# A float32 stage of a tuned FFT-convolution and MLP kernel, remade as three float32r products whose moving halves are split on ScalarE and VectorE

## The chip, the cores and the metric

The kernel runs on one core of one Trainium2 chip. The metric is the device time of one execution in microseconds (us); lower is better.

## The reference, cut to what matters

```python
X = np.fft.rfft(x, axis=1)                      # x: 8 x 3008 x 256, float32
Y = X * (filt_r + 1j * filt_i)[None, :, :]
y = np.fft.irfft(Y, n=3008, axis=1)
h = y.reshape(8 * 3008, 256) @ w_in             # 256 x 2048
P = a[0] + a[1] * h + a[2] * h**2 + a[3] * h**3
Q = 1.0 + abs(b[0]) * abs(h) + abs(b[1]) * h**2
out = (P / (Q + 1e-6)) @ w_out                  # 2048 x 256
```

## The kernel before, in words

The length 3008 is 64 x 47. A batch's convolution has three stages. Stage 1 is the 47-point transform: inputs are folded (a sum or a difference of two mirrored halves, `fold`) and multiplied on TensorE by a 120 x 120 constant (`half_sb`). Stage 2 is the 64-point transform, the filter and the way back. Stage 3 is the inverse 47-point transform, which writes `xhl`, the input of the MLP, as a high and a low float32r part.

The MLP runs over 47 tiles of 512 tokens and, in each, 16 slices of 128 hidden features: a *unit*, 753 in all (the last two steps are halved). A unit has six matmuls into `h_u` (L706 to L709, `product_in`), the rational function on ScalarE, VectorE and GpSimd, and six matmuls out of `hi_u` and `lo_u` (L797 to L799, `product_out`). The names in the rows:

- ScalarE: `act0` L714 (reads `h_u`, writes `q_u`), `act4` L739, `act2` L727, `act1` L721, `act3` L731, five of 128x512 a unit.
- VectorE: `g_hi` L763, `rest` L771, `p` L754, `g_lo` L777, four a unit; each has `h_u`, which lies in PSUM, as one input and an SBUF tile as another.
- GpSimd: `pool_m` L768 and `pool_q1` L749, two a unit, all operands in SBUF.

All compute engines run in the order in which the program is written (`manual_schedule`), and an iteration of the loop in `pipeline` writes out the parts of several units: `in` of unit i, a step of the convolution on TensorE, `out` of an older unit, `g_hi` of i-2, `act3` of i-1, `act0` of i, the convolution step's work on the other engines (`conv_out`), `act4` of i-1, `act2` and `act1` of i, `rest` of i-3, `p` of i-1, `g_lo` of i-3, `pool_m` of i-2, `pool_q1` of i-1. A step of the convolution is let in when a credit of 0.38 an iteration has paid for the step before; its cost is the number that the generator yields (0.86 for a half of stage 1).

The second batch's stage 1 (`stage1`, `b == 1`) and that of the third to eighth (`b` of 2 to 7) are the same generator. It has 13 steps, two for each of six input tiles and one for the seventh. In a step TensorE multiplies one folded half in plain float32 (L519), ScalarE writes the high part (L473, over the input tile `xin`), VectorE the low part (L475, tile `yl`, reads PSUM and `xin`), GpSimd folds the half that is needed two steps later (L456, tile `xs`), and after a tile's last half two DMAs store it. PSUM has six banks (`Banks`) for `h_u` and the convolution; the bank free for longest is taken next.

Rings of SBUF tiles (`RING`) hold the units' values: `q=5` lets `act0` of unit i write a tile that `rest` of unit i-5 was the last to read.

`product3` (L422) multiplies two operands, each given as a high and a low float32r part, by three matmuls: high x high, low x high, high x low. Stage 2 uses it already.

Of the kernel before, what the change touches and what calls it, by code (L numbers as in the profile page):

```python
# [9 lines left out]
F32 = mybir.dt.float32  # L10
F32R = mybir.dt.float32r
I32 = mybir.dt.int32
U32 = mybir.dt.uint32
AF = mybir.ActivationFunctionType
ALU = mybir.AluOpType
# [12 lines left out]
R0 = NB * K2  # L28
SW = 448
AB = 432  # L30
C = 256
# [3 lines left out]
RATES = 0.6, 0.38  # L35
EARLY = 60
XF = 1
RING = dict(a=4, w=3, q=5, hi=5, lo=4)
GAP = 4
PGAP, XGAP = 1, 1  # L40
OG = 2
# [5 lines left out]
XB, FB, YB = 4, 3, 3  # L47
# [9 lines left out]
REST = 2  # L57
# [2 lines left out]
WARM2 = (3, 3, 3, 3)  # L60
DUE = 5
SPN = 1
HEAD_SP = {mybir.EngineType.SP}
SQ0 = 624
SQP = "PA"
# [3 lines left out]
TT = 512  # L69
# [58 lines left out]
class Plan:  # L128
# [10 lines left out]
    def add(self, name, fn, engine, busy, after=(), due=0.0, moves=0.0, bank=None, ring=None, twin=None, then=(), filler=False, pick=None):  # L139
        self.steps.append((name, fn, engine, busy, list(after), due, moves, bank, ring, twin, then, filler, pick))  # L140
# [49 lines left out]
def conv_moe(ctx: ExitStack, tc: tile.TileContext, xp, filt, w_in, w_out, mats, small, sgn, outT):  # L190
    nc = tc.nc
    B = xp.shape[0]

    consts = ctx.enter_context(tc.tile_pool(name="consts", bufs=1))
    dram = ctx.enter_context(tc.tile_pool(name="dram", bufs=3, space=DRAM))
    conv = ctx.enter_context(tc.tile_pool(name="conv", bufs=2))
    mlp = ctx.enter_context(tc.tile_pool(name="mlp", bufs=1))
# [9 lines left out]
    fwd32_sb = consts.tile([128, 128], F32, name="fwd32_sb")  # L207
    small_sb = consts.tile([128, SW], F32, name="small_sb")
    half_sb = [small_sb[:R0, h * R0 : h * R0 + R0] for h in range(2)]
    e_sb = small_sb[:, 2 * R0 : 2 * R0 + 4 * N2]  # L210
    scal = consts.tile([128, 64], F32, name="scal")
    ab_sb, abs_sb, cf_sb = small_sb[:, AB : AB + 12], scal[:, 12:24], scal[:, 24:40]
# [3 lines left out]
    ts, tt, stt = v.tensor_scalar, v.tensor_tensor, v.scalar_tensor_tensor  # L216
# [105 lines left out]

    slots = [f"{x}{k}" for k in range(5) for x in ("a", "w", "q", "hi", "lo") if k < RING[x]]

    class Weights:
# [12 lines left out]
        def load(self):  # L338
            i = self.i
            tag = self.tag  # L340
            bufs = {"raw": 1, "xin": XB, "f1": FB, "f2": FB}.get(tag)
            if tag == "tl":
                raw = conv.tile([128, 4 * C], U32, tag=tag, name=f"raw{i}").rearrange("p (c t) -> p c t", t=2)
            else:
                raw = conv.tile([128, TT, 2], U32, tag=tag, name=f"raw{i}", **({"bufs": bufs} if bufs else {}))
            self.l, self.h = raw[:, :, 0], raw[:, :, 1]
            nc.sync.dma_start(raw.rearrange("p c t -> p (c t)"), self.src)
# [71 lines left out]
    def product3(out, parts, hi, lo):  # L419

        for n, (a, b) in enumerate(((0, hi), (1, hi), (0, lo))):
            nc.tensor.matmul(out, parts[:, a], b, start=n == 0, stop=n == 2)  # L422

    class Banks:
# [6 lines left out]
        def tile(self, name):  # L431
            k = min(self.free, key=self.free.get)
            del self.free[k]
            return k, ps.tile([128, TT], F32, tag=f"h{k}", name=name)
# [6 lines left out]
    def width(t):  # L441
        return TT if t < 6 else C

    def stage1_load(b, t, tile=None):
        n = width(t)
        if tile is None:
            tile = conv.tile([128, 2, n], F32, tag="xin", name=f"xin{b}_{t}", bufs=XB)
        nc.sync.dma_start(
            tile.rearrange("p a b -> p (a b)"),
            xp[b, 2 * TT * 128 * t : (2 * TT * t + 2 * n) * 128].rearrange("(p c) -> p c", p=128),  # L450
        )
        return tile

    def fold(engine, h, out, xin):

        engine.tensor_tensor(out=out, in0=xin[:R0, 0], in1=xin[:R0, 1], op=(ALU.add, ALU.subtract)[h])  # L456

    def stage1_store(issuer, b, t, parts):

        n = width(t) // C  # L460
        for of, part in zip(parts, range(2)):
            slots = scr1[b][part].rearrange("k (b j) r c -> (k b) j r c", j=NJ)[:, 2 * t : 2 * t + n]
            of = of if of.dtype == F32 else of.bitcast(F32)
            issuer.dma_start(slots.rearrange("p j r c -> p (j r c)"), of[:R0, : 2 * n * C])

    def stage1_evict(t, h, parts, pt):

        if t < 6:
            in_ = pt[:R0].rearrange("p (j c) -> p j c", j=2)
            hi, *low = (of[:R0].rearrange("p (j r c) -> p j r c", j=2, r=2)[:, :, h] for of in parts)  # L470
        else:
            in_, (hi, *low) = pt[:R0], (of[:R0, :TT] for of in parts)
        nc.scalar.activation(hi, in_, AF.Copy)  # L473
        for lo in low:
            tt(out=lo, in0=in_, in1=hi.bitcast(F32), op=ALU.subtract)  # L475

    def half_dfts(t, h):
        return [(h, slice(0, TT))] if t < 6 else [(g, slice(g * C, g * C + C)) for g in range(2)]

    def stage1(b, t0=0):  # L480
        tiles, xins = {}, {}

        def load(t):
            if t < 7:
                xins[t] = stage1_load(b, t)

        def prepare(t, h):
            if t > 6:
                return
            if h == 0:  # L490
                load(t + 1)
                xin, n = xins.pop(t), width(t)
                sums = conv.tile([R0, 2, n], F32, tag="ev", name=f"xs{b}_{t}")
                tiles[t] = sums, xin
            sums, xin = tiles[t]
            fold(nc.gpsimd, h, sums[:, h], xin)

        load(t0)
        for _ in range(REST if b == 1 else 1):
            yield 0.01  # L500
            yield
        for h in range(2):
            prepare(t0, h)
            yield
        yield 0.01
        yield
        for t in range(t0, 7):
            sums, xin = tiles.pop(t)
            flat = xin.rearrange("p a b -> p (a b)")
            if b == 1:  # L510
                parts = (flat,)
            else:
                low = conv.tile([128, 4 * C], F32R, tag="yl", name=f"yl{b}_{t}", bufs=YB)
                parts = flat.bitcast(F32R), low
            for h in range(2 if t < 6 else 1):
                yield 0.86
                k, pt = banks.tile(f"s1_{b}_{t}_{h}")
                for g, cs in half_dfts(t, h):
                    nc.tensor.matmul(pt[:R0, cs], half_sb[g], sums[:, g], start=True, stop=True)  # L519
                yield  # L520
                stage1_evict(t, h, parts, pt)
                banks.done(k, 0.5)
                prepare(t + 1, h)
            stage1_store(nc.sync, b, t, parts)

    class Stage2:

# [159 lines left out]
    class Unit:  # L687
# [7 lines left out]
        def tile(self, tag, dt=F32):  # L695
            full = mlp.tile([128, TT], dt, tag=f"{tag}{self.i % RING[tag]}", name=f"{tag}_u{self.i}")
            return full[:, self.cols]
# [103 lines left out]
    banks = None  # L801
# [19 lines left out]
    whole, parts = slice(0, T), [slice(c, c + T // LAST) for c in range(0, T, T // LAST)]  # L821
# [1 line left out]
    units[-TAIL:] = [(t, f, c) for t, f, _ in units[-TAIL:] for c in parts]  # L823

    def conv_items(b):
        yield from stage1(b)
        for _ in range(GAP):
            yield
        yield from stage2(b)
# [6 lines left out]
    def head():  # L836
# [3 lines left out]
        first, sums, pts, yts, zts, pair = {}, {}, {}, {}, {}, []  # L840
# [10 lines left out]
            nc.sync.dma_start(sgn_sb[:, :K2], sgn)  # L851

        def load_pair():
            tile = mlp.tile([128, TT], F32, tag=slots[20], name="pair")
            nc.sync.dma_start(tile, mats.rearrange("p m c -> p (m c)"))
            pair.extend(tile[:, k * 128 : k * 128 + 128] for k in range(4))

# [118 lines left out]
        add = plan.add  # L976
        due = lambda i: DUE + 2.6 * i
        for t in range(7):
            add(f"x{t}", lambda t=t: x_load(t), "SP", 0.5, due=-20 + t, moves=1.55 if t < 6 else 0.78, ring=(("xin", "xin", "xin", "xin", "oe", "oe", "tl")[t], f"sum{min(2 * t + 1, 12)}"))
            if t == 0:  # L980
                add("small", lambda: nc.sync.dma_start(small_sb, small), "SP", 0.5, due=-19.5, moves=0.7)
        add("mats", load_mats, "SP", 0.5, due=-10, moves=0.05)
        add("pair", load_pair, "SP", 0.5, due=-9, moves=0.8)
        add("fwd32", load_fwd32, "SP", 0.5, ["s12"], due=60, moves=0.2)
        add("mats_upper", mats_upper, "ACT", 0.97, ["pair", "sev12"], due=45)
# [30 lines left out]
        for k, i in enumerate(FIRST):  # L1016
            w, n = weights[i], f"w{i}"
# [19 lines left out]
        def split():  # L1037
            nonlocal xh, xl
            xhl = consts.tile([128, 4, RX], F32R, tag="xhl", name="xhl")
            xh, xl = xhl[:, :2], xhl[:, 2:]  # L1040
# [24 lines left out]
    def pipeline(squares):  # L1065
# [10 lines left out]
        for i in range(n + LAG + 2 * OG):  # L1076
# [10 lines left out]
            if i == 0:  # L1087
                sp.enter_context(tc.manual_schedule(engines=HEAD_SP))
            for k in SOON.get(i, ()):
                weights[k].load()  # L1090
            if i == SPN:
                sp.close()
# [86 lines left out]
    with tc.manual_schedule(engines=ENGINES):  # L1179
        with tc.manual_schedule(engines=HEAD_SP):  # L1180
            banks = Banks(range(8 - T * 2 // TT))
# [85 lines left out]
```

## Time and profile before

| | |
|---|---|
| median of 3 runs | 2452.14 us (2450.94 to 2453.37) |
| the profiled execution | 2452.45 us, span 2450.3 us |
| TensorE clock granted | 0.999 |
| TensorE, VectorE, ScalarE, GpSimd busy | 99%, 89%, 91%, 87% |

The span is the time from the first to the last instruction; the 2.15 us around it belong to the execution's time but to no engine. Busy time is the union of an engine's instructions. A matmul's end is modelled and reaches into the next matmul's start, so TensorE's pace is read from the distance between starts; the same holds for ScalarE and VectorE where one instruction follows another without idle time.

### The profile page before, as it was taken

The numbers are of one execution on the slowest core, as the hardware profiler recorded it, in microseconds if no ns is written. First come the engines' busy times: TensorE is split into PE (matmuls) and PEld (weight loads), VectorE is DVE, ScalarE is ACT, GpSimd is POOL, SyncE is SP. The second block draws the span as 40 slices with busy tenths as digits, with TensorE's granted clock in tenths as the row PEclk, the third lists the DMA queues.
The fourth block names the chain that finished last, engine by engine and source line by source line (L and its number), as shares of the span: only waits on it lengthen the run. The fifth ranks groups of instructions, "written<-read, shape, count | busy, mean of one in ns | idle before, by whom it ended". The sixth has DMA issues, their size and how long they took to land.

```text
span 2450.3 us, 36825 instructions
## 1 busy us (share of the span) xinstructions
PE 2419.5 (99%) x10868; PEld 1949.4 (80%) x10868; DVE 2188.6 (89%) x3554; ACT 2231.9 (91%) x4275; POOL 2138.8 (87%) x2240
## 2 busy tenths in 40 slices
PE   9899999999999999999999999999999999999998
PEld 5578778888788887888788877888788888888887
DVE  7988988999899988998899988889899998998998
ACT  6899999999999999999899999999999999888887
POOL 7889987999789987999779997899879987889898
PEclk9999999999999999999999999999999999999999
DMA  7543344333443234432343334333343210100000
GB/s 263 174 130 97 104 137 133 111 90 94 127 145 106 87 108 132 125 104 81 113 158 106 98 99 133 126 100 94 100 133 117 64 38 18 34 26 17 21 9 20
DMA packets 127502, 243.30 MB, mean 99 GB/s; under 512 B 10803, under 2 KB 75763, under 8 KB 127291
## 3 DMA queue, kind: packets, MB, share of 16 engines
q1 hardware_dynamic: 127207, 240.77, 31.8%
q8 instruction: 88, 1.44, 0.3%
q14 instruction: 123, 1.01, 0.1%
q10 hardware_dynamic: 84, 0.08, 0.0%
HBM read 149.47 MB, written 91.34 MB: 98 GB/s over the span
## 4 chain that ended last, share of the span: by engine, by line
PE 72%; POOL 14%; DVE 7%; issue 4%; ACT 2%; DMA 1%; SPq 0%; POOLq 0%; DVEq 0%; ACTq 0%
PE o L798 10%; PE o L797 10%; PE o L799 10%; PE h_u L706 10%; PE h_u L707 10%; PE h_u L709 10%; POOL q_u L768 6%; POOL q_u L749 4%; PE x L665 3%; PE s L519 3%; DVE h_u L771 2%; POOL zw L580 2%; PE z L422 2%; DVE hi_u L763 1%; DVE h_u L754 1%
## 5 line engine op out<-in xcount | busy, mean ns | idle before, releaser
L768 POOL TENSOR_TENSOR q_u<-q_u,hi_u 128x512 f32<-128x512 f32 x753 | 977.0, 1297 | 198.2 <-DVE hi_u L763 174.8
L771 DVE SCALAR_TENSOR_TENSOR h_u<-h_u,q_u 128x512 f32<-128x512 f32 x753 | 523.0, 695 | 124.7 <-POOL q_u L768 123.4
L797 PE MATMUL o<-hi_u,wo_sb 128*128 128x512 f32 x1506 | 633.5, 421 | 0.0
L706 PE MATMUL h_u<-xhl,wi_sb 128*128 128x512 f32 x1506 | 590.9, 392 | 9.7 <-DVE lo_u L777 4.5
L798 PE MATMUL o<-lo_u,wo_sb 128*128 128x512 f32 x1506 | 587.8, 390 | 3.7 <-DVE lo_u L777 3.7
L799 PE MATMUL o<-hi_u,wo_sb 128*128 128x512 f32 x1506 | 586.6, 390 | 0.1
L707 PE MATMUL h_u<-xhl,wi_sb 128*128 128x512 f32 x1506 | 586.1, 389 | 0.2 <-DVE xhl L681 0.2
L749 POOL TENSOR_SCALAR q_u<-q_u,scal 128x512 f32<-128x512 f32 x753 | 580.8, 771 | 4.1 <-ACT a_u L731 4.1
L714 ACT ACTIVATE q_u<-h_u 128x512 f32<-128x512 f32 x753 | 451.6, 600 | 134.1 <-PE h_u L709 105.7
L754 DVE SCALAR_TENSOR_TENSOR h_u<-w_u,scal,h_u 128x512 f32<-128x512 f32 x753 | 563.4, 748 | 3.2 <-ACT w_u L721 3.2
L763 DVE SCALAR_TENSOR_TENSOR hi_u<-h_u,a_u 128x512 fp32r<-128x512 f32 x753 | 515.2, 684 | 3.7 <-ACT a_u L739 3.4
L777 DVE TENSOR_TENSOR lo_u<-h_u,a_u 128x512 fp32r<-128x512 f32 x753 | 516.9, 686 | 0.3
L731 ACT ACTIVATE a_u<-q_u 128x512 f32<-128x512 f32 x753 | 477.8, 635 | 0.0
L727 ACT ACTIVATE q_u<-q_u 128x512 f32<-128x512 f32 x753 | 472.9, 628 | 1.8
L709 PE MATMUL h_u<-xhl,wi_sb 128*128 128x512 f32 x1506 | 463.7, 389 | 0.0
L721 ACT ACTIVATE w_u<-h_u 128x512 f32<-128x512 f32 x753 | 446.3, 593 | 0.0
L739 ACT ACTIVATE a_u<-a_u 128x512 f32<-128x512 f32 x688 | 433.1, 629 | 0.3
L706 PEld LDWEIGHTS h_u<-xhl,wi_sb 128*128 128x128 f32 x1506 | 282.6, 188 | 80.2 <-DVE lo_u L777 16.3
L798 PEld LDWEIGHTS o<-lo_u,wo_sb 128*128 128x128 f32 x1506 | 283.3, 188 | 79.4 <-issue 20.9
L797 PEld LDWEIGHTS o<-hi_u,wo_sb 128*128 128x128 f32 x1506 | 282.9, 188 | 74.4 <-issue 20.5
L799 PEld LDWEIGHTS o<-hi_u,wo_sb 128*128 128x128 f32 x1506 | 282.7, 188 | 60.7 <-POOL wo_sb L401 0.5
L707 PEld LDWEIGHTS h_u<-xhl,wi_sb 128*128 128x128 f32 x1506 | 282.7, 188 | 59.2 <-issue 0.7
(125 smaller groups left out, 2262.3 us busy)
## 6 DMA issues: line engine op xcount, KB each, us to landing
f<-filt SPq DMA_DIRECT2D x168, 256.0 KB
xin<-xp SPq DMA_DIRECT2D x48, 512.0 KB
scr<-ev SPq DMA_DIRECT2D x47, 512.0 KB
outT<-oe SPq DMA_DIRECT2D x46, 512.0 KB
xin<-scr SPq DMA_DIRECT2D x42, 512.0 KB
scr<-xin SPq DMA_DIRECT2D x42, 480.0 KB
yl<-scr SPq DMA_DIRECT2D x36, 512.0 KB
tl<-scr SPq DMA_DIRECT2D x94, 192.0 KB
```

Of the source, the lines that this page charges most:

```text
L706: nc.tensor.matmul(o, w_in_part(0, f, cc), xh[:, cc, ts], start=cc == 0, stop=False)
L707: nc.tensor.matmul(o, w_in_part(0, f, cc), xl[:, cc, ts], start=False, stop=False)
L709: nc.tensor.matmul(o, w_in_part(1, f, cc), xh[:, cc, ts], start=False, stop=cc == 1)
L749: nc.gpsimd.tensor_scalar(out=self.q, in0=self.q, scalar1=S1, scalar2=S2, op0=ALU.mult, op1=ALU.add)
L754: v.scalar_tensor_tensor(out=H, in0=w, scalar=PK, in1=H, op0=ALU.add, op1=ALU.mult)
L763: nc.vector.scalar_tensor_tensor(out=self.hi, in0=self.H, scalar=self.p0, in1=self.a, op0=ALU.add, op1=ALU.mult)
L768: nc.gpsimd.tensor_tensor(out=self.q, in0=self.q, in1=self.hi.bitcast(F32), op=ALU.mult)
L771: nc.vector.scalar_tensor_tensor(out=self.H, in0=self.H, scalar=self.p0, in1=self.q, op0=ALU.add, op1=ALU.subtract)
L777: nc.vector.tensor_tensor(out=self.lo, in0=self.H, in1=self.a, op=ALU.mult)
L797: nc.tensor.matmul(o, w_out_part(0, f, dd), self.hi, start=f == 0 and self.cols.start == 0, stop=False)
L798: nc.tensor.matmul(o, w_out_part(0, f, dd), self.lo, start=False, stop=False)
L799: nc.tensor.matmul(o, w_out_part(1, f, dd), self.hi, start=False, stop=f == 15 and self.cols.stop == T)
```

## The change

Stage 1 of batches three to eight has a generator of its own, `stage1_parts`. Its folds go to a new ring of two float32 tiles (`sh`). One step ahead of its use each folded half is split: ScalarE copies it into a float32r tile (high part), VectorE subtracts that from the folded half (low part). Both operands of this subtraction and its result lie in SBUF. The constant is split likewise, once, into `half_r`, 2,048 bytes of a partition. The float32 matmul becomes `product3`. The ring `q` goes from five tiles to four, and `pair`, a constant of the head, moves into a tile of `sh`.

```diff
-RING = dict(a=4, w=3, q=5, hi=5, lo=4)
+RING = dict(a=4, w=3, q=4, hi=5, lo=4)
+SH = 2
+    half_r = consts.tile([128, 2, 2, 128], F32R, name="half_r")
...
-        for _ in range(REST if b == 1 else 1):
+        for _ in range(REST):
...
+    def half_parts():
+        f = small_sb[:R0, : 2 * R0].rearrange("p (h c) -> p h c", h=2)
+        hi, lo = (half_r[:R0, k, :, :R0] for k in range(2))
+        nc.scalar.activation(hi, f, AF.Copy)
+        tt(out=lo, in0=f, in1=hi.bitcast(F32), op=ALU.subtract)
+
+    def stage1_parts(b):
+        xins, sums, parts, low = {}, {}, {}, {}
+        last = 12
...
+        def add(k):
+            if k > last:
+                return
+            t, h = divmod(k, 2)
+            if h == 0:
+                load(t + 1)
+            sums[k] = conv.tile([R0, TT], F32, tag="sh", name=f"sh{b}_{k}", bufs=SH)
+            for g, cs in half_dfts(t, h):
+                fold(nc.gpsimd, g, sums[k][:, cs], xins[t])
+
+        def split(k):
+            if k > last:
+                return
+            x = sums.pop(k)
+            parts[k] = tile = conv.tile([R0, 2, TT], F32R, tag="ev", name=f"xs{b}_{k}")
+            nc.scalar.activation(tile[:, 0], x, AF.Copy)
+            tt(out=tile[:, 1], in0=x, in1=tile[:, 0].bitcast(F32), op=ALU.subtract)
+
+        load(0)
+        if b == 2:
+            half_parts()
+        yield 0.01
+        yield
+        add(0)
+        yield
+        split(0)
+        add(1)
+        yield
+        yield 0.01
+        yield
+        for k in range(last + 1):
+            t, h = divmod(k, 2)
+            yield 0.86
+            bank, pt = banks.tile(f"s1_{b}_{t}_{h}")
+            tile = parts.pop(k)
+            for g, cs in half_dfts(t, h):
+                w = half_r[:R0, :, g, :R0]
+                product3(pt[:R0, cs], w, tile[:, 0, cs], tile[:, 1, cs])
+            yield
+            if h == 0:
+                low[t] = conv.tile([128, 4 * C], F32R, tag="yl", name=f"yl{b}_{t}", bufs=YB)
+            out = xins[t].rearrange("p a b -> p (a b)").bitcast(F32R), low[t]
+            stage1_evict(t, h, out, pt)
+            banks.done(bank, 0.5)
+            split(k + 1)
+            add(k + 2)
+            if h or k == last:
+                stage1_store(nc.sync, b, t, out)
...
-        yield from stage1(b)
+        yield from stage1(b) if b == 1 else stage1_parts(b)
...
-            tile = mlp.tile([128, TT], F32, tag=slots[20], name="pair")
+            tile = conv.tile([128, TT], F32, tag="sh", name="pair", bufs=SH)
```

## Rows read from the trace of the kernel before

**Rows 1.** The page's part 1: busy us of each engine, share of the span, instructions.

```profile
PE 2419.5 (99%) x10868; PEld 1949.4 (80%) x10868; DVE 2188.6 (89%) x3554; ACT 2231.9 (91%) x4275; POOL 2138.8 (87%) x2240
```

**Rows 2.** Timeline of TensorE in batch three's stage 1: start, length, engine, line.

```profile
363.00 0.39 PE L706 MATMUL h_u<-xhl,wi_sb 128*128 128x512 f32 x1
363.23 0.39 PE L707 MATMUL h_u<-xhl,wi_sb 128*128 128x512 f32 x1
...
365.72 0.39 PE L706 MATMUL h_u<-xhl,wi_sb 128*128 128x512 f32 x1
...
367.08 1.02 PE L519 MATMUL s<-xs,small_sb 120*120 120x512 f32 x2
...
369.32 0.39 PE L706 MATMUL h_u<-xhl,wi_sb 128*128 128x512 f32 x1
```

**Rows 3.** Busy time in the six stage-1 stretches of batches three to eight.

```profile
331.20:407.80 76.60, 76.38 (x329) 59.14 (x328) 66.79 (x108) 69.49 (x132) 59.50 (x58) 1.00 0.36 112
...
sum 443.90, PE 443.05 PEld 342.02 DVE 387.13 ACT 404.04 POOL 351.01; mean PE 73.84 PEld 57.00 DVE 64.52 ACT 67.34 POOL 58.50
```

**Rows 4.** Groups of instructions by line and shape: busy us, mean ns, idle before.

```profile
L456 POOL TENSOR_TENSOR xs<-xin 120x512 f32<-120x512 f32 x84 | 108.7, 1293 | 0.0
...
L519 PE MATMUL s<-xs,small_sb 120*120 120x512 f32 x168 | 86.4, 594 | 2.6 <-DVE raw L390 1.2 <-DVE yl L475 0.9 <-DVE lo_u L777 0.5
...
L475 DVE TENSOR_TENSOR yl<-s,xin 120x512 fp32r<-120x512 f32 x78 | 53.9, 691 | 46.5 <-ACT xin L473 46.5
L590 ACT ACTIVATE zr<-f 128x512 fp32r<-128x512 f32 x84 | 52.9, 630 | 9.2 <-POOL f L584 8.2
```

**Rows 5.** Timeline of ScalarE in the same stretch.

```profile
364.68 0.60 ACT L714 ACTIVATE q_u<-h_u 128x512 f32<-128x512 f32 x1
365.16 0.64 ACT L739 ACTIVATE a_u<-a_u 128x512 f32<-128x512 f32 x1
365.68 0.64 ACT L727 ACTIVATE q_u<-q_u 128x512 f32<-128x512 f32 x1
```

**Rows 6.** Timeline of VectorE in the same stretch.

```profile
362.78 0.69 DVE L475 TENSOR_TENSOR yl<-s,xin 120x512 fp32r<-120x512 f32 x1 [1.71 <-ACT xin L473]
363.38 0.69 DVE L771 SCALAR_TENSOR_TENSOR h_u<-h_u,q_u 128x512 f32<-128x512 f32 x1
...
365.24 0.68 DVE L763 SCALAR_TENSOR_TENSOR hi_u<-h_u,a_u 128x512 fp32r<-128x512 f32 x1
...
367.69 0.68 DVE L763 SCALAR_TENSOR_TENSOR hi_u<-h_u,a_u 128x512 fp32r<-128x512 f32 x1
368.77 0.69 DVE L475 TENSOR_TENSOR yl<-s,xin 120x512 fp32r<-120x512 f32 x1 [0.40 <-ACT xin L473]
```

**Rows 7.** Timeline of GpSimd in the same stretch.

```profile
361.62 1.30 POOL L768 TENSOR_TENSOR q_u<-q_u,hi_u 128x512 f32<-128x512 f32 x1
362.90 0.78 POOL L749 TENSOR_SCALAR q_u<-q_u,scal 128x512 f32<-128x512 f32 x1
...
369.35 1.29 POOL L768 TENSOR_TENSOR q_u<-q_u,hi_u 128x512 f32<-128x512 f32 x1
```

**Rows 8.** Timeline of VectorE in the head of the kernel.

```profile
7.89 6.96 DVE L456 TENSOR_TENSOR xs<-xin 120x512 f32<-120x512 f32 x12 [2.55 <-DMA xin<-xp]
...
21.01 0.83 DVE L377 TENSOR_SCALAR wp<-wt 128x512 uint32<-128x512 uint32 x1
```

**Rows 9.** Timeline of GpSimd in the head of the kernel.

```profile
7.42 0.19 POOL L242 TENSOR_TENSOR scal<-scal 128x1 f32<-128x1 f32 x1
...
8.78 0.48 POOL L245 TENSOR_TENSOR scal<-scal 128x6 f32<-128x6 f32 x1
...
11.71 0.67 POOL L250 TENSOR_TENSOR scal<-scal 128x2 f32<-128x2 f32 x1
```

**Rows 10.** The view of waits: us in total, times, longest us.

```profile
DVE yl L475 <- ACT xin L473: 46.5, 66, 2.1
...
PEld h_u L706 <- DVE lo_u L777: 16.3, 30, 1.7
```

More of the change, by code (lines that the diff above doesn't have):

```diff
@@ L509, in stage1 @@
             flat = xin.rearrange("p a b -> p (a b)")
[L510 to L514, printed above, removed]
+            parts = (flat,)
             for h in range(2 if t < 6 else 1):
@@ L524, in stage1, with load @@
             stage1_store(nc.sync, b, t, parts)
+    def half_parts():
[6 more added lines that the diff above has]
+        last = 12
+        def load(t):
+            if t < 7:
+                xins[t] = stage1_load(b, t)
+        def add(k):
[44 more added lines that the diff above has]
+                stage1_store(nc.sync, b, t, out)
     class Stage2:
```

## Prediction

> **What bounds the kernel now.** I read the page's busy shares first. TensorE is busy for 99% of the span, VectorE, ScalarE and GpSimd for 89, 91 and 87% [rows 1]: one engine leads and three follow closely, so time taken off TensorE counts only as far as the next engine has room. A busy TensorE is not yet a TensorE at its pace, so the timeline came next. In batch three's stage 1 matmuls start 0.23 us apart (363.00, 363.23), the twelve of a unit without a convolution step take 365.72 - 363.00 = 2.72 us, and a unit with a stage-1 half takes 369.32 - 365.72 = 3.60 us [rows 2]. TensorE works without a gap there and sets the pace; a float32 half costs it 3.60 - 2.72 = 0.88 us. (The 594 ns in the view by line are the modelled length of one of its two records [rows 4] and are no price.)
>
> The change touches six stretches, the stage 1 of batches three to eight, 78 halves. I measured them together: 443.9 us, in which TensorE is busy for 443.1, ScalarE for 404.0, VectorE for 387.1, GpSimd for 351.0 [rows 3]. The room is thus 39.9 us on ScalarE, 56.8 on VectorE, 92.9 on GpSimd. The change sends work to the first two.
>
> **What it takes off TensorE.** Three float32r matmuls at 0.227 us (2.72 / 12) are 0.68 us, against 0.88: 0.20 us a half. The seventh tile has two 256-column pieces, six short matmuls for four; I count it like the others, six of 78. Together 78 x 0.20 = 15.6 us: TensorE then needs 443.9 - 15.6 = 428.3 us in the six stretches. The third weight load of a half runs beside the matmuls, as the unit's loads do.
>
> **What it adds to ScalarE.** A copy of 120x512 from SBUF to SBUF for each half. The nearest row is L590, the same copy for stage 2: 0.63 us by itself [rows 4]; in a row ScalarE instructions start 0.48 and 0.52 us apart [rows 5], so 0.52: 78 x 0.52 = 40.6. Need: 404.0 + 40.6 = 444.6 us. That is too high by as much as the instructions now end in idle time: the first stretch has 132 in 69.49 us [rows 3], 0.526 each, and one after the other they take about 0.51. At that the old ones need 404.0 x 0.51 / 0.526 = 391.7 and all 432. So 432 to 445, 437 taken.
>
> **What it adds to VectorE.** A 120x512 subtraction a half. L475 lasts 0.69 us [rows 4] and the next instruction follows 0.60 us after its start (362.78, 363.38) [rows 6]: 78 x 0.60 = 46.8, need 387.1 + 46.8 = 433.9 us. The 46.5 us in which VectorE now waits at L475 for ScalarE's high part [rows 10] lie inside its idle time; they shrink when VectorE is the late one, since ScalarE's copy is then done, so I add nothing for them. With that alone both engines would need a little more than TensorE (428) and less than now (443.9).
>
> **The port.** The new subtraction is unlike every other VectorE instruction of these stretches: those have an operand in PSUM, it has both in SBUF. The trace has such instructions in its head: twelve folds by VectorE, back to back from 7.89 to 14.85 [rows 8]. GpSimd's tiny instructions take 0.19 us just before; beside the folds they take 0.48 and 0.67, the step of the folds (6.96 / 12 = 0.58) [rows 9]. So GpSimd waits there for a VectorE instruction with two SBUF inputs. In the other direction one row hints at it: an instruction of VectorE with SBUF on both sides lasted 0.83 us at 21.01 [rows 8], where 0.69 is usual for its size; GpSimd was at work on SBUF then. The Trainium skill (SBUF — State Buffer, "Who interferes with whom") states the rule: a VectorE instruction with two SBUF inputs and a GpSimd instruction that reads SBUF exclude each other, and whichever starts first holds the shared pair for its whole length. By that rule the sum is the forecast below; without it, it is the first rival. The trace agrees for GpSimd's side.
>
> In these stretches GpSimd is busy for 351.0 of 443.9 us, and its instructions are long. How long would the subtraction wait? It comes right behind L475. At least nothing; at most a whole L768, 1.28 us (361.62 to 362.90) [rows 7]. Two places can be read off. At 363.38 it would find L749 at work until 362.90 + 0.78 = 363.68: 0.30 us. At 368.77 + 0.60 = 369.37 L768 has just begun, 1.26 us to go [rows 6, 7]. In the second VectorE came late by only 0.40 us of waiting for ScalarE. Once VectorE sets the pace, the phase can be worked out: GpSimd starts L768 when L763 is done, then L749, then the fold, 1.28 + 0.78 + 1.29 = 3.35 us [rows 4, 7]; VectorE's next L763 is done 2.45 us later (365.24, 367.69), L475 takes 0.60, so the subtraction is ready at 3.05 and waits for 0.30 us [rows 6]. I take 0.30, where the calculation and the first place meet: 78 x 0.30 = 23.4, and VectorE needs 433.9 + 23.4 = 457.3 us. Half of a long instruction, 0.64, would make it 484; nothing, 433.9. GpSimd loses up to 0.60 us a half, 47 us, and has 92.9.
>
> So VectorE takes TensorE's place as the bound: 457.3 - 443.9 = 13.4 us more. Not all of it reaches the end. VectorE may leave a stretch late and catch up in stage 2, where it has room (its share over the span is 89%). How late is limited by the ring.
>
> **The ring of four.** `act0` of unit i must now come after `rest` of i-4 instead of i-5. At 364.68 it follows the `rest` that ended at 363.38 + 0.69 = 364.07, by 0.61 us [rows 5, 6]; that is the slack that is left, where the ring of five had a unit's time more. As long as VectorE is no later than now it costs nothing: the distance covers it. Behind the waiting `act0` stand ScalarE's high part of the convolution and `act4`, which VectorE wants next, so a VectorE later by more than 0.6 us holds ScalarE as well. I credit 0.6 us for each stretch, 6 x 0.6 = 3.6. A second limit is close to it: TensorE's first matmul of a unit already waits for L777 to free a bank, 16.3 us in 30 places [rows 10], and the subtraction puts every L777 behind it 0.6 us later.
>
> **At nothing.** The folds stay on GpSimd, same number, same time of issue; only their tile changes. Each half is split a step, two iterations, after its fold, so ScalarE finds it done. The stores and loads are the same and stand where they stood in SP's queue. `half_parts` is one small instruction on each of two engines, once. `pair` changes its tile in the head, with nobody behind it in the new ring until batch three. The yields are the same, so the pacing by credit is unchanged.
>
> **Sum**, against the profiled execution (2452.45; span 2450.3 and 2.15 around it, 0.3 above the median of 2452.14, inside the runs' spread): 2452.45 + 13.4 - 3.6 = 2462.2, say 2462 us.
>
> **Rivals.** *No port.* If the subtraction and GpSimd run side by side, or VectorE's wait is near nothing, ScalarE needs 437 us and VectorE 433.9: 443.9 - 437 = 7 us gained, 2445. For it: no row shows VectorE held by a long GpSimd instruction for certain. Against it: GpSimd is plainly held in the head. *TensorE alone.* If the rings let all engines slide into stage 2, the whole 15.6 us come: 2437. Against it: ScalarE and VectorE both need more than 428. *A wash.* Port waits of some 0.1 us: VectorE needs 433.9 + 7.8 = 441.7, and lost phases eat the rest, 2452. The point between the signs is a wait of (443.9 + 3.6 - 433.9) / 78 = 0.17 us a half: above it the kernel is slower. *Long waits.* At 0.64 us a half, VectorE needs 484 us: 2452.45 + 40.1 - 3.6 = 2489; it needs the phase of the second place, L768 begun just ahead of the subtraction, in half of the steps.
>
> **Chances.** Forecast (waits of 0.2 to 0.5 us) 0.45; long waits 0.11; wash 0.17; no port 0.22; TensorE alone 0.05. A change of 0.2%, 4.9 us, is what a measurement of this kernel can tell from none. Slower by that: the forecast and long waits, 0.55, less the forecast's weak end, plus as much from the wash. Same: 0.17. Faster: no port and TensorE alone, 0.27, and 0.01 of the wash. The forecast's own range is 2454 to 2478 (0.2 and 0.5 us of wait: +2.0 and +25.4). For eight in ten I go from 2442 (below it TensorE alone and the best of no port) to 2482 (above it most of the long waits).
>
> **What the profile after should show.** Three float32r matmuls a half in L519's place, a unit with a half down from 3.60 to about 3.4 us of TensorE work, yet the six stretches longer, about 453 us, with idle time on TensorE that VectorE's L777 ends. VectorE's new subtraction longer than 0.69 us, near 1.0 (the wait is inside its length or ahead of it), GpSimd's L768 and L749 longer on the mean in these stretches and the same elsewhere. VectorE's busy time up by some 60 to 75 us, ScalarE's by 40, and VectorE's wait at the eviction's low part well below 46.5. Right and wrong part at the subtraction: at 0.69 us, with VectorE below 95% in the stretches, the port was the wrong step, and the time should come out near 2445. ScalarE waiting for L771 at `act0` in all stages would say that the ring of four costs more than I gave it. If stage 2 shortens or lengthens, my sum over stretches was too narrow.

## The result, and the profile after

The kernel became slower: 2477.68 us (2476.86 to 2478.96) against 2452.14 in runs on the same chip, a ratio of 1.0105 (95% interval [1.0094, 1.0116], given in the same way below), or 25.5 us. The forecast of 2462 had the sign and the mechanism, and made it less than half as large as it is. The profiled execution took 2478.96 us with a span of 2477.2, 26.9 above the span of before.

First the page's busy shares (us, share of the span, instructions), which answer to [rows 1].

```profile
PE 2428.6 (98%) x10952; PEld 1957.5 (79%) x10952; DVE 2272.2 (92%) x3633; ACT 2257.4 (91%) x4354; POOL 2178.0 (88%) x2240
```

VectorE gained 83.6 us of busy time, GpSimd 39.2, although GpSimd was given no work. The six stage-1 stretches of batches three to eight, measured as in [rows 3], show where. A stretch runs from the start of its first stage-1 matmul to the end of ScalarE's part of its last eviction; the columns are stretch, length, busy us (and instructions) of TensorE, its weight loads, VectorE, ScalarE and GpSimd, then the TensorE clock granted, the share of the DMA engines and GB/s.

```profile
331.60:412.70 81.10, 77.00 (x341) 59.69 (x340) 80.21 (x119) 73.84 (x144) 65.06 (x57) 1.00 0.36 108
...
sum 470.90, PE 451.14 PEld 349.05 DVE 466.58 ACT 430.78 POOL 382.02; mean PE 75.19 PEld 58.18 DVE 77.76 ACT 71.80 POOL 63.67
```

443.9 us became 470.9, 27.0 more: the whole growth of the span lies here. VectorE is busy for 466.6 of them. It was 387.1 of 443.9 before, when TensorE had less than 1 us of gaps; now VectorE has 4.3, and TensorE stands idle for 19.8. The work between the stretches, from the end of batch two's stage 1 to the start of the sixth stretch, adds up to 1214.2 us before and after (the differences between the ends and starts of the stage 1 of batches two to eight), so nothing was caught up and nothing lost there.

The groups by line and shape (busy us, mean ns, idle before) answer to [rows 4].

```profile
L555 DVE TENSOR_TENSOR xs<-sh,xs 120x512 fp32r<-120x512 f32 x78 | 96.8, 1241 | 6.5 <-ACT xs L554 6.5
...
L477 DVE TENSOR_TENSOR yl<-s,xin 120x512 fp32r<-120x512 f32 x78 | 52.8, 677 | 4.4 <-ACT xin L475 4.2
```

```profile
L554 ACT ACTIVATE xs<-sh 120x512 fp32r<-120x512 f32 x78 | 49.9, 640 | 0.0
```

```profile
L830 POOL TENSOR_TENSOR q_u<-q_u,hi_u 128x512 f32<-128x512 f32 x751 | 990.0, 1318 | 189.8 <-DVE hi_u L825 167.0 <-POOL xs L458 0.4
L811 POOL TENSOR_SCALAR q_u<-q_u,scal 128x512 f32<-128x512 f32 x751 | 602.1, 802 | 4.4 <-ACT a_u L793 4.4
```

L555 is the new subtraction, L477 the low part of the eviction (L475 before). They have the same shape and both subtract; the one with a PSUM operand takes 0.68 us, the one with both operands in SBUF 1.24. On GpSimd, L830 and L811 were L768 and L749 in the kernel before:

```profile
L768 POOL TENSOR_TENSOR q_u<-q_u,hi_u 128x512 f32<-128x512 f32 x751 | 975.5, 1299 | 198.1 <-DVE hi_u L763 174.8 <-POOL a_u L737 0.4
L749 POOL TENSOR_SCALAR q_u<-q_u,scal 128x512 f32<-128x512 f32 x751 | 579.7, 772 | 4.1 <-ACT a_u L731 4.1
```

They take 36.9 us more together: there the other side of the same exclusion shows. Of the 78 subtractions 72 lie in the stretches; the first of each batch is done before its stretch begins. The windows with the subtraction alone:

```profile
331.60:412.70 81.10, 16.02 (x12) 1.00 0.36 108
...
sum 470.90, DVE 92.13; mean DVE 15.35
```

The view of the tile `sh` has the spread of the subtraction (ns, shortest, median, longest).

```profile
L555 DVE TENSOR_TENSOR xs<-sh,xs x78: 692/1368/1811, 317.4 to 1832.8; 120x512 fp32r<-120x512 f32 x78
```

The timelines of VectorE and GpSimd show two of them (start, length, in brackets the idle time ahead). They answer to [rows 6, 7].

```profile
366.33 0.67 DVE L825 SCALAR_TENSOR_TENSOR hi_u<-h_u,a_u 128x512 fp32r<-128x512 f32 x1
366.93 0.67 DVE L477 TENSOR_TENSOR yl<-s,xin 120x512 fp32r<-120x512 f32 x1
367.53 1.47 DVE L555 TENSOR_TENSOR xs<-sh,xs 120x512 fp32r<-120x512 f32 x1
368.91 0.69 DVE L833 SCALAR_TENSOR_TENSOR h_u<-h_u,q_u 128x512 f32<-128x512 f32 x1
...
373.82 0.67 DVE L477 TENSOR_TENSOR yl<-s,xin 120x512 fp32r<-120x512 f32 x1
374.42 1.04 DVE L555 TENSOR_TENSOR xs<-sh,xs 120x512 fp32r<-120x512 f32 x1
```

```profile
367.15 1.30 POOL L830 TENSOR_TENSOR q_u<-q_u,hi_u 128x512 f32<-128x512 f32 x1 [0.68 <-DVE hi_u L825]
368.42 1.22 POOL L811 TENSOR_SCALAR q_u<-q_u,scal 128x512 f32<-128x512 f32 x1
...
373.61 1.31 POOL L458 TENSOR_TENSOR sh<-xin 120x512 f32<-120x512 f32 x1
374.88 1.74 POOL L830 TENSOR_TENSOR q_u<-q_u,hi_u 128x512 f32<-128x512 f32 x1
376.61 0.77 POOL L811 TENSOR_SCALAR q_u<-q_u,scal 128x512 f32<-128x512 f32 x1
```

The first subtraction is issued at 367.53, when L830 has been at work since 367.15 and has 0.92 us to go; it lasts 1.47 us, 0.78 more than 0.69. L811, next on GpSimd, then lasts 1.22 instead of 0.77. The second is issued at 374.42, 0.50 us before the fold L458 ends, and lasts 1.04, so it waits 0.35; L830, next on GpSimd, lasts 1.74 instead of 1.30. Whoever comes second waits for the other's end, inside its own length, in both directions. VectorE's two waits are each some 0.15 us shorter than what GpSimd's instruction had left. The Trainium skill (SBUF — State Buffer, "SBUF: two separate sides") has this as an exclusive lock on a shared pair of ports, held by whoever issues first for the whole instruction; the trace agrees, with waits of 0.78 and 0.35 us for VectorE and 0.45 and 0.44 for GpSimd in these four rows, but for those 0.15 us.

ScalarE's new wait for `rest` (L833) can be seen in its timeline, which answers to [rows 5], and in the view of waits (us, times, longest), which answers to [rows 10].

```profile
369.70 0.60 ACT L776 ACTIVATE q_u<-h_u 128x512 f32<-128x512 f32 x1 [0.79 <-DVE h_u L833]
```

```profile
POOL q_u L830 <- DVE hi_u L825: 167.0, 190, 3.6
...
ACT q_u L776 <- DVE h_u L833: 45.1, 84, 1.3
PEld h_u L768 <- DVE lo_u L839: 43.7, 76, 1.7
...
PE h_u L768 <- DVE lo_u L839: 13.9, 19, 1.3
PEld s L424 <- DVE xs L555: 12.6, 18, 1.0
```

TensorE's weight load for the first matmul of a unit (line 768, 706 before) waits for VectorE's `g_lo` (line 839, 777 before) in 76 places for 43.7 us; it was 30 places and 16.3 us. VectorE's 46.5 us at the low part of the eviction have shrunk to 4.2.

### The profile page after: what moved, and what is told of

Same layout as the page of the kernel before. It is cut to its first block, busy times and chain, and to the rows that moved or that the text cites. A ratio compares the mean times of both kernels' runs of the same rounds, so it can differ in the third digit from the quotient of the medians.

```text
span 2477.2 us, 37242 instructions
## 1 busy us (share of the span) xinstructions
PE 2428.6 (98%) x10952; PEld 1957.5 (79%) x10952; DVE 2272.2 (92%) x3633; ACT 2257.4 (91%) x4354; POOL 2178.0 (88%) x2240
## 3 DMA queue, kind: packets, MB, share of 16 engines
q8 instruction: 89, 1.46, 0.3%
## 4 chain that ended last, share of the span: by engine, by line
PE 59%; DVE 18%; POOL 14%; issue 5%; ACT 2%; DMA 1%; DVEq 0%; POOLq 0%; SPq 0%; ACTq 0%
PE h_u L768 9%; PE o L860 8%; PE o L859 8%; PE h_u L771 8%; PE h_u L769 8%; PE o L861 8%; POOL q_u L830 6%; DVE h_u L833 4%; POOL q_u L811 4%; DVE h_u L816 3%; DVE hi_u L825 3%; PE x L727 3%; DVE xs L555 3%; POOL zw L642 1%; PE z L424 1%
## 5 line engine op out<-in xcount | busy, mean ns | idle before, releaser
L830 POOL TENSOR_TENSOR q_u<-q_u,hi_u 128x512 f32<-128x512 f32 x753 | 991.4, 1317 | 189.9 <-DVE hi_u L825 167.0
L833 DVE SCALAR_TENSOR_TENSOR h_u<-h_u,q_u 128x512 f32<-128x512 f32 x753 | 519.3, 690 | 120.7 <-POOL q_u L830 119.5
L768 PE MATMUL h_u<-xhl,wi_sb 128*128 128x512 f32 x1506 | 595.5, 396 | 18.3 <-DVE lo_u L839 13.9
L811 POOL TENSOR_SCALAR q_u<-q_u,scal 128x512 f32<-128x512 f32 x753 | 603.3, 801 | 4.4 <-ACT a_u L793 4.4
L859 PE MATMUL o<-hi_u,wo_sb 128*128 128x512 f32 x1506 | 606.5, 403 | 0.0
L861 PE MATMUL o<-hi_u,wo_sb 128*128 128x512 f32 x1506 | 587.3, 390 | 0.1
L825 DVE SCALAR_TENSOR_TENSOR hi_u<-h_u,a_u 128x512 fp32r<-128x512 f32 x753 | 510.0, 677 | 3.3 <-ACT a_u L801 3.0
L768 PEld LDWEIGHTS h_u<-xhl,wi_sb 128*128 128x128 f32 x1506 | 283.1, 188 | 104.9 <-DVE lo_u L839 43.7
```

The lines of the kernel that those rows point to most:

```text
L768: nc.tensor.matmul(o, w_in_part(0, f, cc), xh[:, cc, ts], start=cc == 0, stop=False)
L811: nc.gpsimd.tensor_scalar(out=self.q, in0=self.q, scalar1=S1, scalar2=S2, op0=ALU.mult, op1=ALU.add)
L825: nc.vector.scalar_tensor_tensor(out=self.hi, in0=self.H, scalar=self.p0, in1=self.a, op0=ALU.add, op1=ALU.mult)
L830: nc.gpsimd.tensor_tensor(out=self.q, in0=self.q, in1=self.hi.bitcast(F32), op=ALU.mult)
L833: nc.vector.scalar_tensor_tensor(out=self.H, in0=self.H, scalar=self.p0, in1=self.q, op0=ALU.add, op1=ALU.subtract)
L859: nc.tensor.matmul(o, w_out_part(0, f, dd), self.hi, start=f == 0 and self.cols.start == 0, stop=False)
```

## The experiments

Each run has its ratio to the kernel before on the same chip. My theory: the subtraction, waiting for GpSimd's port, makes VectorE the bound. The rivals that were left: the subtraction as plain work of VectorE, the ring of four, ScalarE's copy.

**Neither part of the split: TensorE's work alone.** The fold writes a float32r tile, which is taken for both parts.

```diff
+                fold(nc.gpsimd, g, sums[k][:, 0, cs], xins[t])
...
-            nc.scalar.activation(tile[:, 0], x, AF.Copy)
-            tt(out=tile[:, 1], in0=x, in1=tile[:, 0].bitcast(F32), op=ALU.subtract)
...
-                product3(pt[:R0, cs], w, tile[:, 0, cs], tile[:, 1, cs])
+                product3(pt[:R0, cs], w, tile[:, 0, cs], tile[:, 0, cs])
```

> The changed kernel without copy and subtraction: GpSimd folds straight into the tile that the three float32r products read, as high and as low part. So the low part is left out of the values; TensorE's work is that of the change. TensorE term: 78 x 0.20 = 15.6 us less than before, 2437 us (2435 to 2440), with everything else as before. Rival (TensorE's saving is lost to other engines anyway): 2445 or more.

2440.51 us against 2452.34, 0.9953 [0.9936, 0.9969]: TensorE's saving is 11.8 us, a little less than I expected. The timeline of TensorE, as in [rows 2], shows the price of a half: the last in-matmuls of three units, a half after the first of them.

```profile
358.94 0.62 PE L768 MATMUL h_u<-xhl,wi_sb 128*128 128x512 f32 x2
359.40 0.87 PE L424 MATMUL s<-xs,half_r 120*120 120x512 f32 x3
...
362.38 0.62 PE L768 MATMUL h_u<-xhl,wi_sb 128*128 128x512 f32 x2
...
365.10 0.62 PE L768 MATMUL h_u<-xhl,wi_sb 128*128 128x512 f32 x2
```

A unit with a half takes 362.38 - 358.94 = 3.44 us, one without 365.10 - 362.38 = 2.72, as before. Three float32r matmuls cost 0.72 us, not 0.68; the saving is 0.16 a half, and 78 x 0.16 = 12.5.

**The copy without the subtraction.** The subtraction goes, and the high part is taken for both.

```diff
-            tt(out=tile[:, 1], in0=x, in1=tile[:, 0].bitcast(F32), op=ALU.subtract)
...
-                product3(pt[:R0, cs], w, tile[:, 0, cs], tile[:, 1, cs])
+                product3(pt[:R0, cs], w, tile[:, 0, cs], tile[:, 0, cs])
```

> The changed kernel with ScalarE's copy and without the subtraction (the high part is read as the low part too, so the low part is left out). ScalarE term: it needs 432 to 445 us in stretches of 444, 437 taken, so 2437 to 2447 us, 2443 as the middle. Rival (ScalarE is full with the copy and alone undoes the saving): 2450 or more.

2440.52 us, 0.9953 [0.9936, 0.9969], the same as without the copy. ScalarE's 78 copies cost nothing. The windows of the six stretches, in the columns used above:

```profile
sum 434.30, PE 432.32 PEld 356.10 DVE 388.28 ACT 426.38 POOL 351.09; mean PE 72.05 PEld 59.35 DVE 64.71 ACT 71.06 POOL 58.52
```

ScalarE is busy for 426.4 of 434.3: it fits, barely. The 437 that I took for it was 10.6 too high; 3.1 of that are the six copies that, like their subtractions, lie ahead of the stretches.

**The subtraction without the rest.** Before, with one 120x512 subtraction of SBUF tiles a half behind the eviction, its result unused.

```diff
+                if b > 1:
+                    spare = conv.tile([R0, TT], F32, tag="spare", name=f"sp{b}_{t}_{h}", bufs=1)
+                    x = sums.rearrange("p a b -> p (a b)")
+                    tt(out=spare, in0=x[:, :TT], in1=x[:, -TT:], op=ALU.subtract)
```

> The kernel before (float32 matmul, ring of five, no copy) with one thing more: in each half of stage 1 of batches three to eight VectorE subtracts two folded halves in SBUF into a spare tile behind L475, where the change has its subtraction. Port theory: VectorE is filled as in the change, 1.2 to 1.3 us an instruction, 2473 to 2482 us. Work theory (it takes the copy, the ring and the subtraction together): 2465 or less.

2490.46 us against 2452.34, 1.0157 [1.014, 1.0174]: 38.1 us, more than I expected. Without the copy, the ring of four and the three products, the subtraction alone costs at least as much as the whole change does, so the cost is the subtraction's. The kernel after has 37.2 us over the run with the copy alone (2477.68 - 2440.52); that the two figures are so close is in part chance. With VectorE as the bound of both, this kernel should take about as long as the kernel after, and it takes 12.8 us longer. Only some 4 of these lie in the stretches, 475.0 us long with VectorE busy for 466.9, and the most of the rest lies between them; here the last subtraction of each batch comes behind its stretch. I did not work out the rest.

```profile
L526 DVE TENSOR_TENSOR sp<-xs 120x512 f32<-120x512 f32 x78 | 104.8, 1343 | 0.0
```

**The same subtraction with an operand in PSUM.** 72 of the 78 subtract the step's PSUM bank in place of the high part, so that the low parts hold other numbers; the work is the same.

```diff
-            tt(out=tile[:, 1], in0=x, in1=tile[:, 0].bitcast(F32), op=ALU.subtract)
+            other = tile[:, 0].bitcast(F32) if pt is None else pt[:R0]
+            tt(out=tile[:, 1], in0=x, in1=other, op=ALU.subtract)
...
+            split(k + 1, pt)
             banks.done(bank, 0.5)
-            split(k + 1)
```

> The changed kernel, but the subtraction takes the step's PSUM bank as its second operand instead of the high part in SBUF (all but the first of each batch), so the low parts hold other numbers; the same count of instructions, same sizes, same places in the order. Port theory: the subtraction lasts 0.69 us instead of 1.24 on the mean, VectorE gets 78 x 0.55 = 43 us back, GpSimd's L830 and L811 lose their long ones, and the time falls to 2442 to 2452 us, bound by ScalarE or TensorE. Work theory (the added copy and subtraction fill ScalarE and VectorE, whatever they wait for): 2468 us or more. Ring theory: 2465 or more.

2447.76 us against 2453.38, 0.9977 [0.9968, 0.9987]: faster than before. First the subtraction in the view of the tile `xs`, then the windows.

```profile
L556 DVE TENSOR_TENSOR xs<-sh,s x72: 671/675/679, 333.5 to 1802.3; 120x512 fp32r<-120x512 f32 x72
```

```profile
sum 439.30, PE 433.68 PEld 353.99 DVE 426.56 ACT 428.30 POOL 352.42; mean PE 72.28 PEld 59.00 DVE 71.09 ACT 71.38 POOL 58.74
```

None of the 72 is longer than 0.68 us, GpSimd is back at 352.4, and VectorE is busy for 426.6 instead of 466.6. The kernel after is 29.9 us slower than this one by the medians (2477.68 - 2447.76; the two ran on different chips, and by their ratios to before it is 31), and the subtraction's operand is the difference, apart from the bank, which is let go after the subtraction here. The 72 also need not wait for ScalarE's copy any more, but that is not it: the wait for the copy is 6.5 us in six places in the kernel after and 6.6 in six here. The result lies in SBUF in both, so it is the second input from SBUF that counts. This is the run that settles the cause. It is still 6 to 7 us slower than the run with the copy alone, though VectorE has 12.7 us of idle time in the stretches; which wait takes these I did not separate.

**The ring.** Before with a ring `q` of four tiles and `pair` in a tile of its own; and after with five, for which the constant's 2,048 bytes had to go and another constant is multiplied.

```diff
-RING = dict(a=4, w=3, q=5, hi=5, lo=4)
+RING = dict(a=4, w=3, q=4, hi=5, lo=4)
```

```diff
-RING = dict(a=4, w=3, q=4, hi=5, lo=4)
+RING = dict(a=4, w=3, q=5, hi=5, lo=4)
...
-    half_r = consts.tile([128, 2, 2, 128], F32R, name="half_r")
...
-                w = half_r[:R0, :, g, :R0]
+                w = fwd_sb[:R0, :, :R0]
```

> The kernel before with the ring q at four instead of five, and pair in a tile of its own; nothing else. Port theory (the subtraction's waits on GpSimd, with VectorE full in the stretches, make the loss): 2451 to 2454 us, because VectorE is late nowhere in the stretches. Ring theory (the ring of four holds ScalarE's act0 behind VectorE's rest and makes the loss, as the 45 us of that wait in the profile after suggest): 2462 us or more.

> The changed kernel with the ring q at five; for the room the constant half_r is left out and another constant's tile is multiplied in its place, so the values differ and the instructions don't. Port theory: VectorE stays full in the stretches, so 2472 to 2478 us, though ScalarE's 45 us of waiting for rest go away. Ring theory: 2465 us or less.

The first took 2452.98 us, 0.9999 [0.9989, 1.0009]; the second 2478.78 against 2453.38, 1.0107 [1.009, 1.0124], as slow as after. In the second, ScalarE's wait at `act0` for `rest`, 45.1 us in after, is not in the view of waits any more, and no time came back. In the first it is there with 13.6 us, at no cost either. It was a wait of an engine that had the time.

**The place: more room between the halves.** One more yield ahead of each next step, so that no unit with a half follows another directly; and before with the same yields as its control.

```diff
+            if k < last:
+                yield
```

> The changed kernel with one more bare yield behind each step of the new stage 1, so that two steps are at least two units apart; the same instructions. Phase theory (a step one unit after another finds GpSimd's L830 just begun behind g_hi and waits for 0.78 us, a step two units after finds the fold's end and waits for 0.35): the subtractions of 1.47 us become 1.05, the mean falls from 1.24 to about 1.05 us, and the time to 2460 to 2468 us. Rival (GpSimd is busy for 79% of these stretches, so the wait is the same wherever the step stands): 1.2 us and 2474 or more.

> The kernel before with the same extra yield in stage 1 of batches three to eight, as a control. Phase theory: 2449 to 2455 us, as nothing waits for a port there. Rival: if the spacing by itself makes the kernel faster by 5 us or more, the run with the spaced change says nothing about phases.

The spaced kernel took 2472.52 us, 1.008 [1.0063, 1.0097]; its control 2464.66, 1.0048 [1.0031, 1.0065]. Both are above what I expected: spacing alone costs 11.3 us, and on it the change costs 7.9 instead of 25.5. The median of the subtraction fell from 1.37 to 1.04 us, as the phase demands, but its mean only from 1.24 to 1.19, where I had expected more:

```profile
L555 DVE TENSOR_TENSOR xs<-sh,xs x78: 702/1044/1908, 316.7 to 1939.7; 120x512 fp32r<-120x512 f32 x78
```

Of the 78, 52 came two units after the one before, and 48 of them took between 1.03 and 1.18, while the 14 that came four units after took 1.46 on the mean. The rest of the smaller cost, I take it without a run that shows it, is room: the six stretches of the control are 569.1 us long, where they were 443.9, and VectorE has over 10 us of idle time in each.

**The place: behind `p`.** The subtraction is put off by an entry of its own, `lows`, behind `('p', 1)` in ORDER: two instructions later in VectorE's order, after `rest` and `p`. In the second run both parts of the split are also made a step earlier.

```diff
+            eng = nc.vector
+            late.append(lambda: eng.tensor_tensor(out=tile[:, 1], in0=x, in1=tile[:, 0].bitcast(F32), op=ALU.subtract))
...
-            own = {"in": unit_in, "pre": conv_in, "out": unit_out, "conv": conv_out}
+            own = {"in": unit_in, "pre": conv_in, "out": unit_out, "conv": conv_out, "lows": lows}
```

```diff
-            split(k + 1)
-            add(k + 2)
+            split(k + 2)
+            add(k + 3)
```

> The changed kernel, not spaced, with VectorE's subtraction written behind p, two instructions later than before; the same instructions. Phase theory: two instructions (1.25 us) after g_hi plus L477 GpSimd is at the end of L830 or in L811, so the wait is 0.2 to 0.4 us instead of 0.55, 2458 to 2468 us, unless TensorE then waits for the low part in the steps one unit apart. Rival (same wait wherever it stands): 2474 or more.

> All subtractions on VectorE behind p, split two steps ahead; the same values. Port theory: VectorE stays the bound with 387 + 78 x 0.85 = 453 us, 2456 to 2464 us; its waits for GpSimd stay, TensorE's for the low part go. Lateness theory for this placement: below 2452.

The first took 2464.91 us against 2453.37, 1.0046 [1.0029, 1.0062], as the phase theory demands: the same subtraction, two instructions later, lasts 0.94 us, and more than half of the loss is gone.

```profile
L562 DVE TENSOR_TENSOR xs<-sh,xs 120x512 fp32r<-120x512 f32 x78 | 73.5, 942 | 0.6 <-ACT xs L560 0.6
```

The second took 2455.64 against 2451.95, 1.0015 [1.0006, 1.0025], just below what the port theory gave. The subtraction lasts 0.99 there, yet TensorE no longer waits for the low part, which it did 17 times in the first:

```profile
PE s L424 <- DVE xs L562: 9.7, 17, 1.3
```

**The other engine.** The subtraction on GpSimd at the end of an iteration; then the odd ones on GpSimd and the even ones on VectorE behind `p`, without and with spacing; then both splits a step earlier.

```diff
+            eng = nc.gpsimd if k % 2 else nc.vector
+            (late if k % 2 else soon).append(lambda: eng.tensor_tensor(out=tile[:, 1], in0=x, in1=tile[:, 0].bitcast(F32), op=ALU.subtract))
```

> The changed kernel with the subtraction on GpSimd, written behind pool_q0 at the end of the iteration; the same values. Port theory: no VectorE instruction of the stretches has two SBUF inputs, so GpSimd's instructions keep their 1.30 and 0.77 us; GpSimd needs 351 + 78 x 1.25 = 449 us of the 444 and becomes the bound: 2452 to 2460 us. Work theory: VectorE loses its load as well, ScalarE's copy stays, 2452 to 2465. Ring theory: VectorE is on time, so the ring does not bind: about 2450.

> The changed kernel, not spaced, every second subtraction on GpSimd at the end of the iteration, the others on VectorE behind p; the same values. Port theory: VectorE and GpSimd have room again (422 and 400 us of 444), but the low part comes late for the steps one unit apart, as with all of them on GpSimd (30 us of TensorE's waiting there, 10 with all of them behind p): 2450 to 2462 us. If the waits for the low part do not show, 2445.

> The changed kernel, spaced, with every second subtraction on GpSimd (at the end of the iteration) and the others on VectorE behind p; the same values. Port theory: VectorE's load in the stretches falls to 387 + 39 x 0.9 = 422 us, GpSimd's rises to 351 + 39 x 1.25 = 400, ScalarE's is 437 and now sets the time: 2444 to 2452 us. Work theory: the time stays above 2460.

> All subtractions on GpSimd at the end of the iteration, as in the earlier run, but each half is split two steps ahead of its use instead of one; the same values. Lateness theory (that run lost its time where TensorE waited for the low part in steps one unit apart): TensorE's waits for it vanish, GpSimd is the fullest engine with 449 us of need, 2446 to 2456 us. Load theory (GpSimd's load made the loss): 2470 or more.

> Every second subtraction on GpSimd at the end of the iteration, the others on VectorE behind p, split two steps ahead; the same values. Lateness theory: no engine needs more than 437 us in the 444, so faster than both kernels, 2442 to 2449 us. Load theory: 2460 or more, as without the second step ahead.

All on GpSimd: 2481.96 us against 2453.38, 1.0113 [1.0096, 1.013], a miss. The port is free (the subtraction takes 1.26 to 1.34 us), but GpSimd is late with it, and the view of waits has a new wait of TensorE:

```profile
PEld s L424 <- POOL xs L562: 42.9, 29, 3.0
PE s L424 <- POOL xs L562: 30.3, 29, 2.6
```

Alternating missed as well, 2473.04 against 2452.34, 1.0085 [1.0068, 1.0101], and has the same wait, 17.9 us in 16 places; with spacing it took 2458.4, 1.0021 [1.0012, 1.0031], 6.3 below its control but above what I expected. With the split a step earlier GpSimd's version fell to 2462.62, 1.0043 [1.0026, 1.0059], above what I expected: TensorE waits 6.1 us for the low part instead of 30.3, but now VectorE's `rest` waits for GpSimd, 164.1 us over the span where it was 123.4 in the kernel before. Alternating and a step earlier took 2451.49 against 2451.95, 0.9998 [0.9988, 1.0008], no change against before where I expected a gain, and so the best version found that has all of the work:

```profile
sum 443.70, PE 436.01 PEld 352.88 DVE 427.16 ACT 426.52 POOL 399.47; mean PE 72.67 PEld 58.81 DVE 71.19 ACT 71.09 POOL 66.58
```

All four engines are busy for 90% or more of these stretches, and the 11.8 us that TensorE could give are gone again; which wait takes them I did not separate. No version ran that beats both kernels with the whole computation.

## Why the prediction was right or wrong

**The mechanism held.** VectorE took TensorE's place as the bound of the six stretches, and GpSimd's port is the cause: the run with a PSUM operand is faster than before by 0.23%, the one with SBUF operands slower by 1.05%. The exclusion works both ways, as the rows above show.

**The step that failed is the port's term**, 0.30 us a half, 23.4 in all. Its measured mean is 1.241 - 0.69 = 0.55, 42.9 in all (40.0 in the stretches, by VectorE's busy time there, 466.58 against 426.56, for the 72 that lie in them). The phase was worked out for a VectorE whose last unit held no half: L763 to L763 in 2.45 us, shorter than GpSimd's round of 3.35, so that the subtraction meets the end of the fold. Where that is so it came out: at 374.42 the wait is 0.35. That the size is so close is in part luck: I had taken the wait to be all that the fold has left, which is 0.50 there, and the wait is 0.15 shorter. But a unit with a half now takes VectorE 2.45 + 0.60 + 1.0 to 1.5, over 4 us, longer than 3.35. If the next unit has a half as well, GpSimd has finished early, waits for `g_hi` (the 0.68 us in brackets at 367.15) and starts L830 the moment that comes; the eviction's low part takes 0.60, and the subtraction finds L830 with 0.92 us to go and waits for 0.78. I counted all 78 by the GpSimd instruction that was running when each was issued: 43 met L830, 31 the fold, 4 L811. Of the 32 that came directly in the next unit, 24 met L830, at 1.48 us on the mean, and 8 the fold's last moments, at 0.76; of the 21 that came two units later, 16 met the fold, at 1.09. So one phase was applied to all steps that holds for those two units apart. The rival "long waits" came nearest: its condition, L830 begun shortly ahead in half of the steps, was met, and the mean of 0.55 lies between the forecast's and its 0.64. Its time, 2489, was too high because the wait and the base below were.

**VectorE's base** was put at 433.9 us without the port; it is 426.6 with the operand in PSUM, 7.3 less. Half of that is a miscount: I put all 78 subtractions into the stretches, where 72 are, and six at 0.60 are 3.6 us. The other 3.7 I take for the ends of VectorE's instructions in idle time, which I had allowed for with ScalarE and not here; no run measured it by itself. On the other side 4.3 us of idle time are left on VectorE. So the sum of 457.3, less 7.3, plus 16.6 for the port (40.0 - 23.4), plus 4.3 gives 470.9, the measured length. The wrong base and the wrong term pulled in opposite directions: with a wait of 0.55 and all else as I had it, the sum would have been 2482.

**The credit of 3.6 us** for lateness caught up in stage 2 did not come: the lengths between the stretches are the same.

**TensorE's term** was 15.6 us and measures 11.8: three matmuls cost 0.72 us. Since TensorE is not the bound after, it changed nothing in the sum; of the rivals only *TensorE alone* used it, and was that much too fast (2437, where the run without the split took 2440.51). The rival *no port*, 2445, is the run with a PSUM operand, at 2447.76.

**ScalarE's copy and the ring at nothing** held, by one run each alone. My sign for the ring was wrong: I had named ScalarE waiting for `rest` at `act0` as proof that it costs more than I gave, and it waits there for 45.1 us, some 32 of them in the six stretches, at no cost.

**What the profile should show** came out in kind: VectorE's busy time up (83.6, where I said 60 to 75), ScalarE's up (25.5, where I said 40: the copies are 49.9, and other instructions are shorter with less idle time), the wait at the eviction's low part nearly gone, TensorE waiting for `g_lo`. The subtraction was to be near 1.0 us and is 1.24, the stretches near 453 and are 470.9.

**Left open**: why the subtractions three to five units after the last one meet L830 as often as they do (14 of 19); I counted them and did not work out their phase. That the wait for TensorE's low part is all that separates the two runs behind `p` was not shown either, since the earlier split also moves the copy and the fold.

## What to carry to other kernels

Before work is given to VectorE beside a busy GpSimd, look where its operands lie: here 78 subtractions cost 6 to 7 us with one operand of 72 of them in PSUM (2447.76 against 2440.52) and 37 with both in SBUF. Size such a wait by the phase after the change, with the new instruction's own length in the period, and for each spacing of the steps, not from one place of the trace before. A wait that appears in the profile is no loss until a run without it is faster.

## What the runs showed of the hardware

The wait for the port is inside the length of the waiting instruction, on either engine: no idle time stands ahead of it, and the engine counts as busy. GpSimd's busy time rose by 39 us with no work added, and in the stretches it fell back from 382.0 to 352.4 when the subtraction had an operand in PSUM. In the two pairs of rows above the subtraction ends about 0.55 us after the GpSimd instruction that it met, 0.14 less than the 0.69 that it takes undisturbed. A GpSimd instruction with one SBUF tile as input (L811, 0.77 to 1.22 us) is held just as one with two is (L830, 1.30 to 1.74).

Three float32r matmuls of 120x512 in a row cost TensorE 0.72 us here, 0.24 each, where those of the units around them stand 0.227 apart.
